# Block attention and two MoE layers on one core: batch 0's scores in plain float32, the softmax sums by a reduce over pairs, and another order of normalising

## Chip, cores and metric

The program runs on one core of a Trainium2 chip. The metric is the device time of one execution in microseconds; the kernel before takes 1253.38 us (median of three runs, 1252.73 to 1253.74).

## What is computed

The reference is an attention block followed by two dense layers of experts. Cut to what matters:

```python
# q, k, v: (4 batches, 8 heads, 576 tokens, 64)
scores = scale * q @ k.T                      # scale = 1/8
mask = (i // 64) >= (j // 64)                 # blocks of 64, causal by block
scores = where(mask, scores, -1e9)
scores = scores - max(scores)
attn = exp(scores)
attn = attn / (sum(attn) + 1e-9)
x = attn @ v                                  # -> (2304, 512)
h = max(x @ w1, x @ w2, x @ w3)               # 512 -> 768
x = h @ w_out                                 # 768 -> 512
p = probs / (sum(probs) + 1e-9)
out = sum over 4 experts: p[:, e] * (relu(x @ w1[e]) @ w2[e])   # 512 -> 1024 -> 512
```

## The kernel before

**Attention.** Two heads make a pair (16 pairs, four per batch). `load_pair` (line 89) brings q and k of a pair to SBUF, transposed, with the 64 head dimensions standing twice, in partitions 0 to 63 and again in 64 to 127. `prep_pair` (line 105) splits them for an exact product out of rounded float32 (fp32r) matmuls: `kk` holds the rounded keys in the lower half of the partitions (line 85 or 87) and the remainders in the upper half (line 122), `q1` the rounded queries times -1/8 (line 133) and `q2` their remainders (line 135). `scores` (line 163) then needs two fp32r matmuls over all 128 partitions per block, one with `q1` and one with `q2` (line 190). Rows of queries go in blocks i of 128; block i sees the keys up to 128(i+1), so blocks 0, 1, 2, 3 have 128, 256, 384 and 512 columns. The last 64 queries of both heads of a pair make one block, i = 4, with 576 columns and four matmuls per stretch. A small bf16 matmul with `corner` (line 195) masks the last 64 columns of blocks 0 to 3. The scores come out negated, so VectorE takes a minimum (line 208), and ScalarE computes exp and, in the same instruction, the row's sum (line 215). `normalise` (line 221) adds 1e-9 (line 223), takes the reciprocal (line 224), both on VectorE, and multiplies each tile on GpSimd (line 226). A head has two groups of tiles: group 0 has blocks 0, 2 and 3 and is normalised in the order 128, 384, 512 keys; group 1 has block 1, and for the second head of a pair block 4 too.

`turn_probs` (line 249) transposes the normalised tiles on TensorE (line 264; 25 transposes per pair) into PSUM. Its first bank of four is taken from block 3, the one with 512 keys, and the second from blocks 2 and 0. VectorE or ScalarE copies a bank to SBUF (lines 273 and 289). Batch 0's values are plain float32 matmuls (`values32`, lines 310, 318 and 322; TensorE runs each as two instructions); batches 1 to 3 use fp32r parts (lines 348 and 359).

**Order.** The loop at line 598 works on head g and on the scores of head g + 2; what `normalise` does is held back by one stage (`stage`, line 576). The framework then schedules the instructions by a simulated timeline, so that an engine can take an instruction that stands much later in the program. The first dense layer (`moe1`, line 526) of batch b needs all heads of the batch; from there on its matmuls (line 505) are mixed with the attention of the batch that follows. Its weights arrive as 64-bit floats and are converted once (`Convert`, line 394) in 26 pieces: ScalarE at lines 429, 431 and 85, GpSimd at lines 436 and 443, VectorE at lines 438, 439 and 452. These pieces already run during batch 0.

**Places.** Pairs 0 and 2 of batch 0 are loaded into `arena`, pairs 1 and 3 into `raw`. The split form of pairs 1 and 3 lies in the tile `spare`, which uses the place of the dense layer's `hh`; that of pairs 0 and 2 lies in `q1`, `q2` and `kk`. PSUM has four one-bank tiles (`ps_x`) for scores and transposes, one two-bank tile (`ps_c`) for block 4, and two banks (`ps_v`) for batch 0's values.

Of the kernel before, what the change touches and what calls it, by code (L numbers as in the profile page):

```python
# [6 lines left out]
F32 = mybir.dt.float32  # L7
# [11 lines left out]
P = 128  # L19
# [2 lines left out]
MOST = (1.875 - 2.0 ** -23) * 2.0 ** 32  # L22


def program(tc, q, k, v, w123, w_out, probs, e_w1, e_w2, out):
    nc = tc.nc

    B, H, D, S = q.shape[0], 2 * q.shape[1], q.shape[2] // 2, q.shape[4]
# [51 lines left out]

    QT, QW = 2 * (S - 64), 2 * S + 64
    pairs, heads, later = {}, {}, []
    def rounded(engine, to, x):
        if engine is nc.scalar:
            engine.copy(to, x)
        else:
            engine.tensor_scalar(to, x, 1.0, 0.0, op0=ALU.mult, op1=ALU.add)

    def load_pair(g):
        b, h0 = divmod(2 * g, H)  # L90

        if g % 2:
            raw = ap_.tile([P, 2, 2, S], F32, name="raw", tag="raw")[:]
        else:
            o = (B - 1) * KD * S
            raw = arena[:, o:o + 4 * S].rearrange("p (n h s) -> p n h s", n=2, h=2)
        for hs in ((0, 1), (1, 2)) if g == 0 else ((0, 2),):
            for n, src in ((1, k), (0, q)):
                nc.sync.dma_start(out=raw[:, n, hs[0]:hs[1]], in_=src[b, h0 // 2, :, hs[0]:hs[1]])

        vraw = ap_.tile([P, 5, 2, D], F32, name="vraw", tag="vraw", bufs=4)
        nc.sync.dma_start(out=vraw, in_=v[b, h0 // 2])
        pairs[g] = dict(raw=raw, vraw=vraw)

    def prep_pair(g):


        raw, vraw = pairs[g]["raw"], pairs[g]["vraw"]
        if g < NPAIR and g % 2:

            spare = mp.tile([P, 2 * QW + 2 * S], F32R, name="spare", tag="hh")
            q1, q2 = spare[:, 0:QW], spare[:, QW:2 * QW]
            kk = spare[:, 2 * QW:].rearrange("x (h s) -> x h s", h=2)
        else:
            q1, q2 = (ap_.tile([P, QW], F32R, name=x, tag=x, bufs=1)[:] for x in ("q1", "q2"))
            kk = ap_.tile([P, 2, S], F32R, name="kk", tag="kk", bufs=1)[:]
        for x in (q1, q2):
            nc.gpsimd.memset(x[:, QT + 64:QT + 128].bitcast(U32), 0)

        def keys(hs):  # L120
            (rounded if g else lambda _, to, x: rounded(nc.vector, to, x))(nc.scalar, kk[:, hs], raw[:, 1, hs])
# [15 lines left out]
        if g == 0:  # L137
            for h in range(2):
                keys(slice(h, h + 1))
                queries(slice(h, h + 1))  # L140
            yield
        else:
            keys(slice(0, 2))
            yield
            queries(slice(0, 2))
        pairs[g].update(q1=q1, q2=q2, kk=kk)
        if g < NPAIR:
            return
# [14 lines left out]
    def scores(g, grp):  # L163
        pair, h = pairs[g // 2], g % 2
        if grp == 0:
            heads[g] = dict(
                p=[None] * 4,
                mn=ap_.tile([P, 5], F32, name="mn", tag="mn", bufs=3),
                sm=ap_.tile([P, 5, 2], F32, name="sm", tag="sm", bufs=3),
            )  # L170
        mn, sm, pt = heads[g]["mn"], heads[g]["sm"][:, :, 0], heads[g]["p"]
        masked = g < 2 * H
        c0 = 3 * grp
        sets = []
        for tag, cols, plan in GROUPS[1][h] if grp else GROUPS[0]:
            st = (ps_x if tag == "x" else ps_c).tile([P, cols], F32, name="st", tag=tag)
            sets.append((st, plan))
            for i, o, w in plan:

                if i == 4:  # L180
                    todo = [(QT + 64 * x, x) for x in range(2)]
                else:
                    todo = [(h * QT // 2 + P * i, h)]
                c = 0
                while c < w:
                    n = min(w - c, 512 - (o + c) % 512)
                    terms = [(part, q0, x) for q0, x in todo for part in ("q1", "q2")]
                    ends = masked and i < 4 and c + n == w
                    for m, (part, q0, x) in enumerate(terms):
                        nc.tensor.matmul(  # L190
                            out=st[:, o + c:o + c + n], lhsT=pair[part][:, q0:q0 + P],
                            rhs=pair["kk"][:, x, c:c + n], start=m == 0, stop=m == len(terms) - 1 and not ends,
                        )
                    if ends:
                        nc.tensor.matmul(
                            out=st[:, o + w - 64:o + w], lhsT=corner, rhs=corner[:, 0:64], start=False, stop=True
                        )
                    c += n
        c = c0
        done = []  # L200
        for st, plan in sets:
# [7 lines left out]
            for col, i, o, w in mine:  # L209
                x = ap_.tile([P, w], F32, name=f"p{i}", tag=f"p{i}", bufs=2 if i == 4 else 3)  # L210
                if i == 4:
                    pair["p4"] = x
                else:
                    pt[i] = x
                nc.scalar.activation(  # L215
                    x, st[:, o:o + w], ACTF.Exp, bias=mn[:, col:col + 1], scale=-1.0,
                    accum_out=sm[:, col:col + 1],
                )
# [1124 lines left out]
```

## Time and profile before

| | |
|---|---|
| median of three runs | 1253.38 us |
| the profiled execution | 1249.91 us, span 1248.1 us |
| granted TensorE clock, mean | 0.996 |
| TensorE busy | 1211.2 us (97%) |
| VectorE busy | 929.7 us (74%) |
| ScalarE busy | 517.8 us (41%) |
| GpSimd busy | 357.1 us (29%) |

The span runs from the first instruction to the last; the 1.8 us between it and the execution's time lie around it. Busy shares are means over stages that have different limits. A matmul's end is modelled: in a stretch where TensorE runs without a gap the start of the next instruction, not the duration shown, tells what one costs.

### The profile page before, as it was taken

The numbers are of one execution on the slowest core, as the hardware profiler recorded it, in microseconds if no ns is written. First come the engines' busy times: TensorE is split into PE (matmuls) and PEld (weight loads), VectorE is DVE, ScalarE is ACT, GpSimd is POOL, SyncE is SP. The second block draws the span as 40 slices with busy tenths as digits, with TensorE's granted clock in tenths as the row PEclk, the third lists the DMA queues.
The fourth block names the chain that finished last, engine by engine and source line by source line (L and its number), as shares of the span: only waits on it lengthen the run. The fifth ranks groups of instructions, "written<-read, shape, count | busy, mean of one in ns | idle before, by whom it ended". The sixth has DMA issues, their size and how long they took to land.

```text
span 1248.1 us, 19730 instructions
## 1 busy us (share of the span) xinstructions
PE 1211.2 (97%) x7417; PEld 1157.8 (93%) x7417; DVE 929.7 (74%) x1716; ACT 517.8 (41%) x1076; POOL 357.1 (29%) x444
## 2 busy tenths in 40 slices
PE   7879998999999999999999999999999999999998
PEld 5669997999999999989999998999999999999998
DVE  7978988666565634377888896758787888686896
ACT  7977767544544421233444441233232223322222
POOL 3957786454344212243333341000000000000000
PEclk9999999999999999999999999999999999999999
DMA  8745574554533488478887864778888887776754
GB/s 304 248 164 197 170 265 161 172 153 155 183 102 119 120 287 304 150 303 332 312 311 296 310 247 162 287 274 316 300 306 311 315 314 281 253 258 228 253 210 170
DMA packets 82644, 299.69 MB, mean 240 GB/s; under 512 B 8748, under 2 KB 18036, under 8 KB 69492
## 3 DMA queue, kind: packets, MB, share of 16 engines
q1 hardware_dynamic: 82548, 298.42, 67.3%
q8 instruction: 59, 0.97, 0.3%
q14 instruction: 37, 0.30, 0.1%
HBM read 215.26 MB, written 83.14 MB: 239 GB/s over the span
## 4 chain that ended last, share of the span: by engine, by line
PE 74%; DVE 10%; DMA 5%; POOL 4%; ACT 3%; issue 3%; SPq 0%; DVEq 0%; ACTq 0%; POOLq 0%
PE m L858 24%; PE m L505 19%; PE o L1017 17%; PE st L190 3%; PE pv L359 2%; PE o L940 2%; PE o L943 2%; PE o L944 2%; DMA t<-in_e_w 2%; PE m L1017 2%; POOL p L226 2%; PE tt L264 2%; DVE mn L208 2%; DMA part<-in_e_w 1%; POOL arena L443 1%
## 5 line engine op out<-in xcount | busy, mean ns | idle before, releaser
L505 PE MATMUL m<-xh,wt 128*128 128x288 f32 x1120 | 238.4, 298 | 0.7 <-ACT mt L541 0.4
L858 PE MATMUL m<-t,w 128*128 128x384 f32 x1152 | 228.5, 336 | 0.0
L1017 PE MATMUL o<-hx,w 128*128 128x384 f32 x1176 | 225.7, 337 | 0.0
L1017 PEld LDWEIGHTS o<-hx,w 128*128 128x128 f32 x1176 | 207.8, 188 | 0.1
L858 PEld LDWEIGHTS m<-t,w 128*128 128x128 f32 x1152 | 203.4, 188 | 2.5 <-DVE tmp L878 0.4
L505 PEld LDWEIGHTS m<-xh,wt 128*128 128x128 f32 x1120 | 183.7, 188 | 1.6 <-DVE mt L543 0.8
L858 PE MATMUL m<-b,w 128*128 128x384 f32 x864 | 175.7, 337 | 2.0 <-ACT tmp L883 2.0
L505 PE MATMUL m<-xl,wt 128*128 128x288 f32 x560 | 165.3, 295 | 0.0
L858 PEld LDWEIGHTS m<-b,w 128*128 128x128 f32 x864 | 153.2, 188 | 5.1 <-ACT tmp L883 2.3
L226 POOL TENSOR_SCALAR p<-p,sm 128x128 f32<-128x128 f32 (+1 forms) x144 | 98.7, 702 | 52.1 <-DVE sm L223 17.0
L505 PEld LDWEIGHTS m<-xl,wt 128*128 128x128 f32 x560 | 105.3, 188 | 0.3
L878 DVE TENSOR_TENSOR tmp<-m,tmp 128x384 f32<-128x384 f32 x144 | 77.9, 550 | 19.4 <-PE m L858 19.2
L505 PE MATMUL m<-hh,wo 128*128 128x288 f32 x384 | 81.3, 299 | 2.9 <-ACT arena L554 1.3
L215 ACT ACTIVATE p<-st,mn 128x128 f32<-128x128 f32 (+3 forms) x144 | 78.5, 555 | 8.2 <-DVE mn L208 6.3
L988 ACT CAST hx<-hq 128x768 fp32r<-128x768 f32 x49 | 40.6, 837 | 99.0 <-PE o L1017 75.9
L190 PE MATMUL st<-kk,q 128*128 128x128 f32 (+4 forms) x336 | 71.2, 340 | 8.7 <-ACT q L133 5.5
L940 PE MATMUL o<-w,hh 128*128 128x512 f32 x192 | 74.7, 391 | 0.9 <-ACT hh L918 0.6
L813 POOL TENSOR_TENSOR w<-part,w 128x512 fp32r<-128x512 f32 x32 | 49.2, 1557 | 91.3 <-ACT w L811 61.2
L943 PE MATMUL o<-w,hh 128*128 128x512 f32 x192 | 74.7, 390 | 0.0
L944 PE MATMUL o<-w,hl 128*128 128x512 f32 x192 | 74.1, 390 | 0.0
L543 DVE TENSOR_TENSOR mt<-m,mt 128x288 f32<-128x288 f32 x96 | 43.2, 452 | 40.3 <-PE m L505 39.9
L264 PE MATMUL tt<-ident,p 128*128 128x128 f32 x400 | 61.0, 278 | 9.8 <-POOL p L226 5.4
(169 smaller groups left out, 2173.8 us busy)
## 6 DMA issues: line engine op xcount, KB each, us to landing
w<-kb SPq DMA_DIRECT2D x55, 1024.0 KB, 6.1
w<-ka SPq DMA_DIRECT2D x30, 1792.0 KB, 7.9
ka<-w SPq DMA_DIRECT2D x16, 1792.0 KB, 6.7
wt<-held SPq DMA_DIRECT2D x54, 512.0 KB, 4.1
kb<-part SPq DMA_DIRECT2D x16, 1024.0 KB, 7.0
kb<-w SPq DMA_DIRECT2D x16, 768.0 KB, 4.7
arena<-in_w SPq DMA_DIRECT2D x18, 512.0 KB, 4.0
wo<-held SPq DMA_DIRECT2D x12, 768.0 KB, 4.5
```

Of the source, the lines that this page charges most:

```text
L190: nc.tensor.matmul(out=st[:, o + c:o + c + n], lhsT=pair[part][:, q0:q0 + P], rhs=pair["kk"][:, x, c:c + n], start=m == 0, stop=m == len(t ...
L215: nc.scalar.activation(x, st[:, o:o + w], ACTF.Exp, bias=mn[:, col:col + 1], scale=-1.0, accum_out=sm[:, col:col + 1],)
L226: nc.gpsimd.tensor_scalar(x, x, sm[:, col:col + 1], 1.0, op0=ALU.mult, op1=ALU.mult)
L264: nc.tensor.transpose(tt[:, c:c + P], pt[i][:, k0:k0 + P], ident)
L505: nc.tensor.matmul(out=out_, lhsT=w, rhs=x, start=m == 0, stop=m == n - 1)
L813: eng.tensor_tensor(w[:, a:b, 1], raw[:, a:b], f(w[:, a:b, 0]), op=ALU.subtract)
L858: ins = nc.tensor.matmul(out=m, lhsT=a, rhs=b, start=start and n == 0, stop=stop and n == 3 * KH - 1, skip_group_check=True,)
L878: nc.vector.tensor_tensor(t, x, y, op=ALU.add)
L940: ins = nc.tensor.matmul(out=o, lhsT=hh[:, ts], rhs=wh, start=i == 0, stop=False)
L943: nc.tensor.matmul(out=o, lhsT=hh[:, ts], rhs=wl, start=False, stop=False)
L944: nc.tensor.matmul(out=o, lhsT=hl[:, ts], rhs=wh, start=False, stop=i == G - 1)
L1017: nc.tensor.matmul(out=o, lhsT=a, rhs=b, start=start and m == 0, stop=stop and m == 2, skip_group_check=True,)
```

## The change

Batch 0's q and k come in a second layout, `qk`: per pair, keys and queries of the first head in partitions 0 to 63 and those of the second head in 64 to 127, so a pair is half as many bytes. All four pairs have places of their own in the tiles `hh` and `hl` of the dense layer. Preparing a pair is a multiplication of the queries by -1/8 in place (VectorE for pair 0, GpSimd for pairs 1 to 3), with the last 64 queries of the two heads put on the diagonal of a zeroed 128 by 128 tile, `last`. A block of scores is then one plain float32 matmul over 64 partitions (128 for block 4). Batches 1 to 3 keep their split form.

For all batches the tile of sums has 1e-9 written beside each sum once, at the start, and one `tensor_reduce` over each pair of numbers gives sum + 1e-9. The tiles of group 0 are normalised in the order 512, 384, 128 keys.

```diff
+    sums = [ap_.tile([P, 5, 2], F32, name=f"sm{n}", tag=f"sm{n}") for n in range(3)]
+    for x in sums:
+        nc.gpsimd.memset(x, 1e-9)
...
     def load_pair(g):
         b, h0 = divmod(2 * g, H)
-        if g % 2:
-            raw = ap_.tile([P, 2, 2, S], F32, name="raw", tag="raw")[:]
+        if g < NPAIR:
+            if g == 0:
+                pairs["hh"] = mp.tile([P, 3, 2, S], F32, name="plain", tag="hh")
+                pairs["hl"] = mp.tile([P, NF, S], F32, name="plain", tag="hl")
+                for n in range(2):
+                    nc.gpsimd.memset(pairs["hl"][:, 2 + n, 0:P].bitcast(U32), 0)
+            raw = pairs["hh"][:, g] if g < 3 else pairs["hl"][:, 0:2]
+            for n in ((0, 1), (1, 2)) if g == 0 else ((0, 2),):
+                nc.sync.dma_start(out=raw[:, n[0]:n[1]], in_=qk[g, :, n[0]:n[1]])
         else:
...
-        for hs in ((0, 1), (1, 2)) if g == 0 else ((0, 2),):
             for n, src in ((1, k), (0, q)):
-                nc.sync.dma_start(out=raw[:, n, hs[0]:hs[1]], in_=src[b, h0 // 2, :, hs[0]:hs[1]])
+                nc.sync.dma_start(out=raw[:, n], in_=src[b, h0 // 2])
...
     def prep_pair(g):
-        if g < NPAIR and g % 2:
-            spare = mp.tile([P, 2 * QW + 2 * S], F32R, name="spare", tag="hh")
...
+        if g < NPAIR:
+            engine = nc.gpsimd if g else nc.vector
+            last = pairs["hl"][:, 2 + g % 2, 0:P]
+            x = raw[:, 1]
+            engine.tensor_scalar(x[:, 0:S - 64], x[:, 0:S - 64], -scale, 0.0, op0=ALU.mult, op1=ALU.add)
+            for half, at in ((lo, 0), (hi, 64)):
+                engine.tensor_scalar(
+                    last[half, at:at + 64], x[half, S - 64:S], -scale, 0.0, op0=ALU.mult, op1=ALU.add
+                )
+            pairs[g].update(k=raw[:, 0], q=x, last=last)
+            yield
+            return
...
     def scores(g, grp):
-                sm=ap_.tile([P, 5, 2], F32, name="sm", tag="sm", bufs=3),
+                sm=sums[g % 3],
...
+                if g < H:
+                    own = both if i == 4 else hi if h else lo
+                    terms = [(pair["last"] if i == 4 else pair["q"][own, P * i:P * i + P], pair["k"][own])]
...
         def normalise():
             cs = slice(c0, c)
-            nc.vector.tensor_scalar(sm[:, cs], sm[:, cs], 1e-9, None, op0=ALU.add)
-            nc.vector.reciprocal(sm[:, cs], sm[:, cs])
-            for col, x in done:
-                nc.gpsimd.tensor_scalar(x, x, sm[:, col:col + 1], 1.0, op0=ALU.mult, op1=ALU.mult)
+            nc.vector.tensor_reduce(mn[:, cs], sm[:, cs], axis=AX.X, op=ALU.add)
+            nc.vector.reciprocal(mn[:, cs], mn[:, cs])
+            for col, x in (done if grp else done[::-1]):
+                nc.gpsimd.tensor_scalar(x, x, mn[:, col:col + 1], 1.0, op0=ALU.mult, op1=ALU.mult)
```

## Rows read from the trace of the kernel before

**Rows 1.** Windows: stretch, length, busy (count) per engine, TensorE clock, DMA share, GB/s.

```profile
0.00:5.50 5.50, 0.00 (x0) 0.00 (x0) 1.22 (x2) 1.92 (x3) 1.27 (x12) 1.00 0.64 193
5.50:88.90 83.40, 69.13 (x372) 52.19 (x372) 70.67 (x141) 70.87 (x187) 57.58 (x74) 0.94 0.70 251
88.90:110.00 21.10, 21.10 (x158) 19.97 (x158) 19.42 (x48) 17.07 (x42) 11.43 (x15) 1.00 0.48 158
110.00:250.00 140.00, 132.82 (x961) 125.55 (x961) 116.68 (x273) 93.91 (x228) 99.68 (x132) 1.00 0.59 194
250.00:1248.10 998.10, 988.12 (x5932) 960.12 (x5930) 721.67 (x1255) 334.02 (x620) 187.19 (x214) 1.00 0.69 248
```

**Rows 2.** Timeline of all engines, 4 to 89 us: start, duration, instruction, idle before.

```profile
4.86 0.78 ACT L133 ACTIVATE q<-arena 128x512 fp32r<-128x512 f32 x2 [2.85 <-DMA arena<-in_q]
...
16.24 1.98 PE L190 MATMUL st<-spare 128*128 128x320 f32 x10 [2.26 <-ACT p L215]
...
18.11 1.95 PE L264 MATMUL tt<-ident,p 128*128 128x128 f32 x8
...
22.16 0.39 PE L310 MATMUL pv<-eh,vraw 128*128 128x128 f32 x2
...
76.34 0.47 PE L310 MATMUL pv<-eh,vraw 128*128 128x128 f32 x2
...
89.00 0.38 PE L505 MATMUL m<-xh,wt 128*128 128x288 f32 x1
```

**Rows 3.** Chain of waits in batch 0: start, length, engine, what, line, count.

```profile
70.35 0.43 PE st L190 x2
...
70.82 2.02 PE pv L318 x8
...
75.87 0.04 PE st L195
75.91 0.55 PE st L190 x2
...
88.22 0.44 PE tt L264 x4
```

**Rows 4.** Groups by line and shape, 0 to 115 us: the split into parts.

```profile
L122 DVE TENSOR_TENSOR spare<-raw,spare 64x1152 fp32r<-64x1152 f32 x2 | 3.7, 1842 | 1.3 <-ACT spare L85 1.3
L135 DVE SCALAR_TENSOR_TENSOR spare<-raw,spare 128x1024 fp32r<-128x1024 f32 x2 | 2.6, 1302 | 0.0
L85 ACT CAST spare<-raw 128x1152 fp32r<-128x1152 f32 x2 | 2.3, 1148 | 0.0
L133 ACT ACTIVATE spare<-raw 128x1024 fp32r<-128x1024 f32 x2 | 2.1, 1062 | 0.0
L122 DVE TENSOR_TENSOR kk<-arena,kk 64x576 fp32r<-64x576 f32 x2 | 1.5, 755 | 0.1
L87 DVE TENSOR_SCALAR kk<-arena 128x576 fp32r<-128x576 f32 x2 | 0.9, 460 | 4.2 <-DMA arena<-in_k 4.1
```

**Rows 5.** Groups by line and shape, 0 to 115 us: normalising and GpSimd.

```profile
L195 PE MATMUL st<-corner 128*128 128x64 bf16 x49 | 10.8, 220 | 0.0
L226 POOL TENSOR_SCALAR p<-p,sm 128x512 f32<-128x512 f32 x12 | 8.8, 731 | 0.0
L226 POOL TENSOR_SCALAR p<-p,sm 128x128 f32<-128x128 f32 x12 | 5.3, 441 | 5.5 <-ACT p L215 2.0 <-ACT wo L85 1.9 <-DVE sm L224 0.9
L223 DVE TENSOR_SCALAR sm<-sm 128x3 f32<-128x3 f32 x12 | 4.6, 387 | 1.3 <-ACT p L215 1.2
L208 DVE TENSOR_REDUCE mn<-st 128x1 f32<-128x128 f32 x12 | 3.4, 280 | 1.1 <-PE st L195 0.9
L224 DVE RECIPROCAL sm<-sm 128x3 f32<-128x3 f32 x12 | 2.1, 172 | 0.2
```

**Rows 6.** Timeline of the last head's wait, 76 to 82 us, columns as in rows 2.

```profile
78.62 2.70 POOL L226 TENSOR_SCALAR p<-p,sm 128x128 f32<-128x128 f32 x3 [1.95 <-ACT wo L85]
...
81.38 0.66 PE L264 MATMUL tt<-ident,p 128*128 128x128 f32 x4 [4.35 <-POOL p L226]
```

More of the change, by code (lines that the diff above doesn't have):

```diff
@@ L22, with program @@
 MOST = (1.875 - 2.0 ** -23) * 2.0 ** 32
-def program(tc, q, k, v, w123, w_out, probs, e_w1, e_w2, out):
+def program(tc, qk, q, k, v, w123, w_out, probs, e_w1, e_w2, out):
     nc = tc.nc
@@ L90, in load_pair @@
         b, h0 = divmod(2 * g, H)
[L92 to L97 removed]
+        if g < NPAIR:
[7 more added lines that the diff above has]
+                nc.sync.dma_start(out=raw[:, n[0]:n[1]], in_=qk[g, :, n[0]:n[1]])
+        else:
+            if g % 2:
+                raw = ap_.tile([P, 2, 2, S], F32, name="raw", tag="raw")[:]
+            else:
+                o = (B - 1) * KD * S
+                raw = arena[:, o:o + 4 * S].rearrange("p (n h s) -> p n h s", n=2, h=2)
             for n, src in ((1, k), (0, q)):
[L99 removed]
+                nc.sync.dma_start(out=raw[:, n], in_=src[b, h0 // 2])
         vraw = ap_.tile([P, 5, 2, D], F32, name="vraw", tag="vraw", bufs=4)
@@ L108, in prep_pair @@
         raw, vraw = pairs[g]["raw"], pairs[g]["vraw"]
-        if g < NPAIR and g % 2:
-            spare = mp.tile([P, 2 * QW + 2 * S], F32R, name="spare", tag="hh")
[L112 to L116, printed above, removed]
+        if g < NPAIR:
[10 more added lines that the diff above has]
+            return
+        q1, q2 = (ap_.tile([P, QW], F32R, name=x, tag=x, bufs=1)[:] for x in ("q1", "q2"))
+        kk = ap_.tile([P, 2, S], F32R, name="kk", tag="kk", bufs=1)[:]
         for x in (q1, q2):
@@ L135, in queries @@
                 nc.vector.scalar_tensor_tensor(low, src, -scale, f(high), op0=ALU.mult, op1=ALU.subtract)
[L137 to L145, printed above, removed]
+        keys(slice(0, 2))
+        yield
+        queries(slice(0, 2))
         pairs[g].update(q1=q1, q2=q2, kk=kk)
-        if g < NPAIR:
-            return
         vs = ap_.tile([P, 2, 5, P], F32R, name="vs", tag="vs", bufs=2)
@@ L168, in scores @@
                 mn=ap_.tile([P, 5], F32, name="mn", tag="mn", bufs=3),
-                sm=ap_.tile([P, 5, 2], F32, name="sm", tag="sm", bufs=3),
+                sm=sums[g % 3],
             )
-        mn, sm, pt = heads[g]["mn"], heads[g]["sm"][:, :, 0], heads[g]["p"]
+        mn, sm, pt = heads[g]["mn"], heads[g]["sm"], heads[g]["p"]
         masked = g < 2 * H
@@ L178, in scores @@
             for i, o, w in plan:
-                if i == 4:
-                    todo = [(QT + 64 * x, x) for x in range(2)]
-                else:
-                    todo = [(h * QT // 2 + P * i, h)]
+                if g < H:
+                    own = both if i == 4 else hi if h else lo
+                    terms = [(pair["last"] if i == 4 else pair["q"][own, P * i:P * i + P], pair["k"][own])]
+                elif i == 4:
+                    terms = [
+                        (pair[part][:, QT + 64 * x:QT + 64 * x + P], pair["kk"][:, x])
+                        for x in range(2) for part in ("q1", "q2")
+                    ]
+                else:
+                    q0 = h * QT // 2 + P * i
+                    terms = [(pair[part][:, q0:q0 + P], pair["kk"][:, h]) for part in ("q1", "q2")]
                 c = 0
@@ L186, in scores @@
                     n = min(w - c, 512 - (o + c) % 512)
-                    terms = [(part, q0, x) for q0, x in todo for part in ("q1", "q2")]
                     ends = masked and i < 4 and c + n == w
-                    for m, (part, q0, x) in enumerate(terms):
+                    for m, (qs, ks) in enumerate(terms):
                         nc.tensor.matmul(
-                            out=st[:, o + c:o + c + n], lhsT=pair[part][:, q0:q0 + P],
-                            rhs=pair["kk"][:, x, c:c + n], start=m == 0, stop=m == len(terms) - 1 and not ends,
+                            out=st[:, o + c:o + c + n], lhsT=qs, rhs=ks[:, c:c + n],
+                            start=m == 0, stop=m == len(terms) - 1 and not ends,
                         )
@@ L1303 @@
         laid[name] = np.concatenate((x, x), axis=2)
+    x = np.stack([inputs[name][0].reshape(H // 2, 2, S, D) for name in ("k", "q")])
+    laid["qk"] = x.transpose(1, 2, 4, 0, 3).reshape(H // 2, P, 2, S)
     x = np.zeros((B, H // 2, 5 * P, 2, D), np.float32)
@@ L1324 @@
     arrays, args = {}, []
-    for name in ("q", "k", "v", "w123", "w_out", "probs", "e_w1", "e_w2"):
+    for name in ("qk", "q", "k", "v", "w123", "w_out", "probs", "e_w1", "e_w2"):
         a = np.ascontiguousarray(laid[name])
```

4 lines of the change are left out of this document (2 added, 2 removed).

## The prediction

> **What bounds the kernel now.** I read the windows first, because the shares over the whole span mix stages. Of the 1248.1 us, TensorE is busy for all but 0.0 us of 88.9 to 110, 7.2 us of 110 to 250 and 10.0 us of the rest [rows 1]. After 88.9 us, therefore, TensorE's own work sets the end, and what the change does there is small. Before, it is different: nothing of TensorE in the first 5.5 us, then 69.1 busy of 83.4 us, beside 70.7 of VectorE, 70.9 of ScalarE and 57.6 of GpSimd [rows 1]. No engine is full, and these four wait for each other in turn. This stretch is batch 0's attention; it ends where the first dense layer's matmul starts, at 89.00 [rows 2]. **If that start moves by a microsecond, the end moves by nearly a microsecond**, since what follows is full. The question is thus when batch 0 is done.
>
> I cut this stretch in three with the timeline [rows 2]: the filling (to the first transpose of head 0, at 18.11), a steady part (first values matmul of head 0 at 22.16, of head 7 at 76.34: seven heads in 54.2 us, 7.74 us each), and the end of head 7 to 89.00.
>
> **TensorE's work per head.** In stretches without gaps the chain of waits gives prices [rows 3]. Eight instructions of line 318 for a first head (widths 384, 384, 256 and 128, two instructions each, nine blocks of 128 columns) take 2.02 us: plain float32 costs 0.224 us per 128 columns. A transpose costs 0.44 / 4 = 0.11. An fp32r block with two terms costs 0.55 for 512 columns and 0.43 for 384, and its mask 0.04; I take 0.3 for 256 and 0.2 for 128 on the same line. A pair before: two heads' blocks 0 to 3, 3.0 us; block 4, 4.5 column blocks by four matmuls at 0.06 (half the step from 384 to 512), 1.1; eight masks, 0.3; 25 transposes, 2.75; 25 column blocks of values, 5.6. Sum 12.8, or 6.4 per head. So of 7.74 us per head about 1.3 are stalls.
>
> **The change, part by part.**
> *Scores in plain float32.* A pair has 20 column blocks plus 4.5, at 0.224: 5.5 us in place of 4.1, so 0.7 us more per head. By columns alone (four passes against two for blocks 0 to 3, the same for block 4) it is 5120 columns at 2.4 GHz, 1.07 per head. I take 0.9, and batch 0 gains 7 us of TensorE work. It costs nothing where it falls into stalls, and all of it where it doesn't.
> *The split goes.* For pairs 1 to 3 ScalarE loses 1.15 + 1.06 us and VectorE 1.84 + 1.30 each; for pair 0 VectorE loses 2 x (0.46 + 0.755) and subtractions like those of line 135 at about half [rows 4]. With the small pieces for the last 64 queries that is near 14 us of VectorE and 9 of ScalarE in a stretch where each is 85% busy. What takes its place is three multiplications per pair. For pair 0 they are on VectorE: the row of 576 columns took 0.46, so 0.45 and two small ones of about 0.2. For pairs 1 to 3 they are on GpSimd: 0.73 for 512 columns and up to 0.44 each for the small ones [rows 5], 1.6 us per pair; the two memsets per pair that go are not counted against it. They are done well ahead, as their loads no longer wait for a place; uncovered they would delay one head's scores by 1.6 us.
> *Loads.* SP issues two transfers for pair 0 in place of four, and one per pair for pairs 1 to 3 in place of two; nothing moves later on its queue. The first two stay as large as before, so keys arrive near 4.1 and queries near 4.86 [rows 2, 4].
> *Filling.* Pair 0's queries are scaled by 5.3, and TensorE can run both heads' scores at once (5.5 us and masks 0.3), to about 11.2; block 4 of pair 1, which the scheduler placed ahead of the first transposes before too (at 16.24 [rows 2]), adds 1. Head 0's 512-key tile needs scores (1.8), a minimum (0.7), exp (0.9), reduce and reciprocal (0.35) and GpSimd (0.73), so it is ready near 10, before TensorE is free. The first transpose comes near 12.5 in place of 18.1: **-5.5 us**. It can't be worth more than about 8 (ready at 10), and 0 if exp still runs in the old order.
> *Sum + 1e-9.* The add of three numbers took 387 ns on average, the reciprocal of the same shape behind it 172 [rows 5]. A reduce of six elements is bounded below by about that reciprocal and above by the 280 of the reduce over 128; I take 0.17, which frees about 0.3 us of VectorE per head, inside the stalls. The page "SBUF — State Buffer" of the Trainium skill (section "SBUF: two separate sides") says that VectorE's two-port modes and GpSimd lock each other out of a shared pair of ports, and "VectorE: DVE Perf Modes" (section "The perf-mode tier table") gives tensor_reduce only the plain mode; by that the reduce wouldn't wait for GpSimd at all, and would sit at the lower bound.
> *Order.* Head 7's transposes waited 4.35 us for three GpSimd tiles of 2.70 us together [rows 6], because the first bank needs the tile that comes last. With it first, four transposes and the first copy run under the other two tiles. That is worth between 0 and 2.70 - 0.73 = 2.0 us at this place, and nothing where TensorE has other work. The clock stood at a mean of 0.94 in this stretch and 1.00 after it [rows 1]; a shorter wait may spare some of that. I take **-1.5 us**.
> *Steady part.* TensorE needs 6.4 + 0.9 = 7.3 per head. If half of the 1.3 us of stalls stay, since VectorE and ScalarE are relieved but the chain through exp, GpSimd and copies is as long, a head takes 7.97: 7 x 0.23 = **+1.6 us**.
> *Afterwards.* Weight pieces converted earlier may spare part of the 7.2 us idle in 110 to 250, or a new order may add to it; I take 0 and keep 3 us each way for the range.
> Sum: -5.5 - 1.5 + 1.6 = -5.4 us. The profiled execution is 1249.91, so it would be 1244.5; it lies 3.5 below the median of the runs, and against the median this is **1248.0 us**.
>
> **Rivals.**
> *A. As summed*, 1248.0; by itself 1244 to 1250.8.
> *B. The stalls go with the work that caused them.* VectorE and ScalarE lose 1.7 and 1.1 us per head, about as much as the stalls. Then TensorE paces at 7.3 per head: -3.1, with filling and end -10.1, so 1243.3, and 1240 with some of the later idle time. For it: TensorE is the only engine that would be near full. Against: GpSimd gains work and its tiles are what TensorE waited longest for.
> *C. Nothing to see.* All 1.3 us of stalls stay, being latencies and weight pieces in the queues, which the scheduler can pull into any freed time. A head takes 8.6: +6.2, less 7.0, so about 1252.6.
> *D. Slower: the array changes height.* Scores over 64 partitions alternate with masks over 128: four such blocks per head, in and out, eight changes. If TensorE must empty itself at each, a change costs what a mask takes alone less what it costs in a full stream, 0.22 - 0.04 = 0.18 us [rows 3, 5], or 1.44 per head. Then 7.3 + 1.44 + 0.65 = 9.4 per head: +11.6 - 7.0 = +4.6, so 1258. It decides from about 1 us per head more than TensorE needs in A. No row shows such a change, since all matmuls before use 128 partitions. The Trainium skill, "TensorEngine Tiling (Array Packing)", section "Key Properties", says that changing the tiling mode drains TensorE; by that D happens, unless the time is hidden in the stalls.
>
> **How the numbers follow.** A measurement of this kernel can tell 0.2%, or 2.5 us, from no change: 1250.9 to 1255.9 counts as the same. Chances: A 0.47, B 0.20, C 0.18, D 0.15. Faster is A and B, 0.67; the same is C, 0.18; slower is D, 0.15. The range goes from B's lower end, 1240, to D's, 1258; A alone has 1244 to 1250.8.
>
> **What would show it.** Right: the first transpose near 12.5 and the first dense matmul near 83.5; no instruction of lines 85, 122, 133 and 135 for batch 0; scores of 512 columns near 0.9 us; the new reduce near 0.17; later windows as full as before. Heads at 7.3 us would be B, at 8.6 C, at 9.4 D. For D the time from a block's last score to the mask behind it must show a gap near 0.18 in every block. The forecast is wrong at its root if the dense layer starts earlier and the end doesn't: then 110 to 250 lost what batch 0 won.

## The result and the profile after

The kernel after takes **1265.01 us** (median of four runs, 1263.04 to 1267.19), beside 1253.06 us of the kernel before (four runs, 1250.26 to 1253.74): a ratio of 1.010 with a 95% interval of 1.0077 to 1.0123. It is slower, and by more than the range reached (1258.0). The profiled execution is the longest of the four, 1267.19 us with a span of 1265.2; its mean granted clock is 0.993, that of the shortest 0.997.

The lines of the code have moved: plain scores are L207, their masks L212, the minimum L225, exp L232, the new reduce L240, the reciprocal L241, GpSimd's normalising L243, transposes L281, batch 0's values L327, L335 and L339, the dense layer L522.

The windows come first (columns as in [rows 1]; the last two rows are parts of the third):

```profile
5.50:88.90 83.40, 80.98 (x322) 46.94 (x321) 53.80 (x116) 58.17 (x160) 49.52 (x69) 1.00 0.58 208
88.90:110.00 21.10, 18.68 (x116) 15.59 (x116) 14.29 (x35) 15.38 (x41) 9.17 (x11) 0.92 0.35 122
110.00:250.00 140.00, 131.84 (x934) 124.90 (x933) 114.33 (x261) 92.37 (x222) 103.00 (x132) 0.96 0.58 195
...
220.00:230.00 10.00, 7.33 (x31) 6.47 (x32) 8.82 (x25) 4.73 (x14) 2.17 (x3) 0.63 0.38 135
230.00:240.00 10.00, 10.00 (x66) 9.87 (x65) 5.31 (x14) 6.18 (x18) 3.57 (x8) 0.86 0.41 137
```

In 5.5 to 88.9 VectorE and ScalarE have fallen from 70.7 and 70.9 us of work [rows 1] to 53.8 and 58.2, but TensorE is now busy for 80.98 of the 83.4 us and issues fewer matmuls in it (322 for 372). The bound of batch 0 has moved from a ring of four engines to TensorE alone. The timeline of TensorE (start, duration, instruction) says why; a cost is read from one start to the next:

```profile
5.16 0.79 PE L207 MATMUL st<-plain 64*128 64x128 f32 x2 [5.16 <-DVE plain L126]
...
17.31 2.07 PE L207 MATMUL st<-plain 64*128 64x512 f32 x2
19.32 0.24 PE L212 MATMUL st<-corner 128*128 128x64 bf16 x1
19.36 1.95 PE L281 MATMUL tt<-ident,p 128*128 128x128 f32 x8
21.24 0.79 PE L207 MATMUL st<-plain 64*128 64x128 f32 x2
...
29.79 0.64 PE L327 MATMUL pv<-eh,vraw 128*128 128x128 f32 x2
...
45.00 1.04 PE L281 MATMUL tt<-ident,p 128*128 128x128 f32 x8
45.97 0.48 PE L207 MATMUL st<-plain 64*128 64x128 f32 x2
46.38 0.20 PE L212 MATMUL st<-corner 128*128 128x64 bf16 x1
46.52 0.91 PE L207 MATMUL st<-plain 64*128 64x384 f32 x2
47.36 0.20 PE L212 MATMUL st<-corner 128*128 128x64 bf16 x1
47.49 1.12 PE L207 MATMUL st<-plain 64*128 64x512 f32 x2
48.55 0.20 PE L212 MATMUL st<-corner 128*128 128x64 bf16 x1
```

**First reading, the clock's level.** Eight transposes take 1.88 us at 19.36 and 0.97 at 45.00; a 512-column block takes 2.01 at 17.31 and 1.06 at 47.49. From 5.16 to about 34 every price is double, which is the lower of the two levels (1.2 GHz), though TensorE doesn't pause once in that stretch. The granted clock of the windows stands at 1.00 there, against the steps. The trace's record of the clock has its first entry only at 34.87 us, and the windows print 1.00 for the time before it. So the step from start to start is what is read; the first entry of the record lies where the steps halve, and it dates the rise of the level below.

The kernel before starts at the lower level too. Its 384 columns in two terms take 0.79 us at 7.03 and 0.44 at 34.12:

```profile
7.03 0.99 PE L190 MATMUL st<-kk,q 128*128 128x384 f32 x2
7.82 0.28 PE L195 MATMUL st<-corner 128*128 128x64 bf16 x1
...
34.12 0.59 PE L190 MATMUL st<-kk,q 128*128 128x384 f32 x2
34.56 0.20 PE L195 MATMUL st<-corner 128*128 128x64 bf16 x1
34.60 0.71 PE L190 MATMUL st<-kk,q 128*128 128x512 f32 x2
```

Its level rose at 13.74. Behind a wait of 2.26 us [rows 2] it was low again from 17.15 to 20.56, and the eight transposes at 18.11 lie in that stretch.

**Second reading, where batch 0's time went.** First values of heads 0, 1 and 7, and the first dense matmul:

| | head 0 | head 1 | head 7 | dense |
|---|---|---|---|---|
| before | 22.16 | 26.95 | 76.34 | 89.00 |
| after | 29.79 | 41.68 | 88.31 | 99.15 |

Up to head 1 it loses 14.7 us. From head 1 to head 7 it gains: 46.63 us for six heads (7.77 each) in place of 49.39 (8.23). The end of head 7 gains 1.8. Together +10.15 when the dense layer starts. Behind that point the profiled span is 1166.05 in place of 1159.1, another +6.95, which includes a drop of the clock to 0.63 at 220 to 230 (more on this under "Afterwards" below).

The small forecasts held: the scores start at 5.16 in place of 5.54, no split instruction of batch 0 is left, and the new reduce is short. The groups of 0 to 115 us (busy us, mean ns of one):

```profile
L241 DVE RECIPROCAL mn<-mn 128x3 f32<-128x3 f32 x11 | 1.9, 169 | 0.2
L240 DVE TENSOR_REDUCE mn<-sm 128x3 f32<-128x6 f32 x11 | 1.7, 154 | 3.3 <-ACT p L232 3.2
```

It takes 154 ns where the add took 387 [rows 5]. That 387 is a mean of two kinds. Of the 24 adds of all widths up to 115 us 12 took 124 to 169 ns; the other 12 took 308 to 637, and each of them ended 0.02 to 0.03 us behind the end of a GpSimd instruction. Of the 24 reduces none took more than 160 ns, though 12 ran beside a GpSimd instruction.

### The profile page after: what moved, and what is told of

It reads as the page before. It is cut to its first block, busy times and chain, and to the rows that moved or that the text cites. A ratio compares the mean times of both kernels' runs of the same rounds, so it can differ in the third digit from the quotient of the medians.

```text
span 1265.2 us, 19665 instructions
## 1 busy us (share of the span) xinstructions
PE 1236.1 (98%) x7401; PEld 1162.8 (92%) x7401; DVE 915.3 (72%) x1702; ACT 508.3 (40%) x1063; POOL 353.3 (28%) x450
## 4 chain that ended last, share of the span: by engine, by line
PE 77%; DVE 10%; DMA 4%; ACT 3%; POOL 3%; issue 2%; SPq 0%; DVEq 0%; POOLq 0%; ACTq 0%
PE m L875 23%; PE m L522 18%; PE o L1034 16%; PE st L207 5%; PE tt L281 2%; PE pv L376 2%; PE o L957 2%; PE o L960 2%; PE o L961 2%; PE m L1034 2%; DMA t<-in_e_w 2%; DVE mn L225 1%; POOL p L243 1%; PE pv L335 1%; DVE tmp L895 1%
## 5 line engine op out<-in xcount | busy, mean ns | idle before, releaser
L522 PE MATMUL m<-xh,wt 128*128 128x288 f32 x1120 | 238.2, 298 | 1.8 <-DVE mt L560 1.1
L522 PEld LDWEIGHTS m<-xh,wt 128*128 128x128 f32 x1120 | 183.6, 188 | 2.8 <-DVE mt L560 1.3
L522 PE MATMUL m<-xl,wt 128*128 128x288 f32 x560 | 165.2, 295 | 0.0
L243 POOL TENSOR_SCALAR p<-p,mn 128x512 f32<-128x512 f32 (+1 forms) x144 | 99.1, 707 | 27.8 <-DVE mn L241 16.5
L522 PEld LDWEIGHTS m<-xl,wt 128*128 128x128 f32 x560 | 105.2, 188 | 0.3
L895 DVE TENSOR_TENSOR tmp<-m,tmp 128x384 f32<-128x384 f32 x144 | 77.7, 549 | 19.5 <-PE m L875 19.3
L232 ACT ACTIVATE p<-st,mn 128x128 f32<-128x128 f32 (+3 forms) x144 | 78.5, 555 | 16.5 <-DVE mn L225 14.4
L522 PE MATMUL m<-hh,wo 128*128 128x288 f32 x384 | 83.2, 303 | 1.9 <-ACT arena L571 1.3
L225 DVE TENSOR_REDUCE mn<-st 128x1 f32<-128x128 f32 (+3 forms) x144 | 66.8, 504 | 19.1 <-PE st L212 16.0
L522 PEld LDWEIGHTS m<-hh,wo 128*128 128x128 f32 x384 | 64.4, 192 | 3.1 <-ACT arena L571 1.5
```

Of the source, the lines that this page charges most:

```text
L225: nc.vector.tensor_reduce(mn[:, col:col + 1], st[:, o:o + w], axis=AX.X, op=ALU.min)
L232: nc.scalar.activation(x, st[:, o:o + w], ACTF.Exp, bias=mn[:, col:col + 1], scale=-1.0, accum_out=sm[:, col, 0:1],)
L243: nc.gpsimd.tensor_scalar(x, x, mn[:, col:col + 1], 1.0, op0=ALU.mult, op1=ALU.mult)
L522: nc.tensor.matmul(out=out_, lhsT=w, rhs=x, start=m == 0, stop=m == n - 1)
L895: nc.vector.tensor_tensor(t, x, y, op=ALU.add)
```

## Experiments

Twelve kernels ran, in three series, each beside the kernel before. All medians, and the milestones of one profiled execution each (first values of heads 0, 1 and 7, first dense matmul, and the span behind it). "Level up" is the first entry of the record of TensorE's clock; "low behind" is how many us behind the first dense matmul the record has at the lower level, without the last 5 us of the span:

| kernel | median us | ratio (95%) | head 0 | head 1 | head 7 | dense | behind | level up | low behind |
|---|---|---|---|---|---|---|---|---|---|
| before | 1253.06 | | 22.16 | 26.95 | 76.34 | 89.00 | 1159.1 | 13.74 | 0 |
| after | 1265.01 | 1.0100 (1.0077 to 1.0123) | 29.79 | 41.68 | 88.31 | 99.15 | 1166.1 | 34.87 | 13.7 |
| rows128 | 1251.34 | 0.9999 (0.9983 to 1.0015) | 18.32 | 27.06 | 75.26 | 83.58 | 1163.6 | 9.09 | 6.8 |
| mask64 | 1259.88 | 1.0059 (1.0044 to 1.0074) | 25.42 | 34.62 | 79.73 | 90.37 | 1165.8 | 24.99 | 10.2 |
| before_mask64 | 1256.15 | 1.0028 (1.0015 to 1.0041) | 25.51 | 30.51 | 83.39 | 95.81 | 1159.5 | 26.53 | 0 |
| warm_up | 1261.28 | 1.0065 (1.0045 to 1.0085) | 26.03 | 38.27 | 84.38 | 92.23 | 1163.8 | 4.55 | 6.8 |
| long_64rows | 1263.66 (one run) | | 38.03 | 47.84 | 91.97 | 99.81 | 1162.1 | 28.83 | 0 |
| norm_only | 1252.00 | 1.0000 (0.9987 to 1.0012) | 22.68 | 28.52 | 79.77 | 87.62 | 1160.4 | 13.43 | 0 |
| scores_only | 1258.84 | 1.0048 (1.0033 to 1.0063) | 29.82 | 40.76 | 87.42 | 95.44 | 1163.0 | 32.97 | 6.8 |
| order_undone | 1260.74 | 1.0058 (1.0041 to 1.0076) | 29.74 | 40.35 | 86.90 | 94.91 | 1162.9 | 32.22 | 3.4 |
| rows128_old_norm | 1250.31 | 0.9980 (0.9970 to 0.9989) | 18.70 | 27.41 | 74.32 | 84.78 | 1163.4 | 8.98 | 6.8 |
| rows128_warm | 1247.16 | 0.9951 (0.9935 to 0.9967) | 18.72 | 27.34 | 74.42 | 82.76 | 1164.0 | 7.63 | 10.2 |
| warm_old_norm | 1252.51 | 0.9996 (0.9986 to 1.0005) | 20.93 | 29.61 | 78.18 | 88.36 | 1162.6 | 9.33 | 3.4 |
| before_warm | 1257.64 | 1.0037 (1.0020 to 1.0055) | 21.11 | 33.23 | 82.82 | 93.39 | 1160.4 | 5.74 | 0 |

**rows128: the same scores over all 128 partitions.** Each head's queries stand in a tile whose other 64 partitions are zero, so the product is the same and no matmul changes height.

```diff
-                    own = both if i == 4 else hi if h else lo
-                    terms = [(pair["last"] if i == 4 else pair["q"][own, P * i:P * i + P], pair["k"][own])]
+                    q0 = h * (S - 64) + P * i
+                    terms = [(pair["last"] if i == 4 else pair["q"][:, q0:q0 + P], pair["k"])]
...
```

Not shown are the memsets of the two zeroed tiles and the multiplication of the queries, which now goes head by head into them.

> The changed kernel with batch 0's scores over all 128 partitions: each head's queries stand in a zeroed tile, the other head's half is zero, and the keys of both heads stream. Columns and passes stay the same; no matmul uses 64 partitions any more. Theory H (the change of height costs 0.2 to 0.3 us per block of scores, 32 blocks): a 512-key block takes 0.85 to 0.95 us at the upper clock instead of 1.06, the first dense matmul starts 6 to 9 us earlier than 99.15, time 1256 to 1259. Theory P (the four passes of plain float32 themselves fill TensorE): a block keeps its price but for a few hundredths, 1262 to 1266. Theory C (64 partitions keep the granted clock at its lower level to 34 us): transposes at 0.11 us already near 20 us, which is worth another 5 us, so 1251 to 1256 together with H.

Measured: 1251.34 us, 13.7 less than after. The timeline of TensorE, columns as above:

```profile
7.17 2.06 PE L214 MATMUL st<-plain 128*128 128x512 f32 x2
9.02 0.24 PE L219 MATMUL st<-corner 128*128 128x64 bf16 x1
9.09 0.68 PE L214 MATMUL st<-plain 128*128 128x256 f32 x2
...
31.26 0.39 PE L214 MATMUL st<-plain 128*128 128x128 f32 x2
31.48 0.19 PE L219 MATMUL st<-corner 128*128 128x64 bf16 x1
31.51 0.89 PE L214 MATMUL st<-plain 128*128 128x384 f32 x2
32.24 0.19 PE L219 MATMUL st<-corner 128*128 128x64 bf16 x1
32.26 1.10 PE L214 MATMUL st<-plain 128*128 128x512 f32 x2
33.21 0.19 PE L219 MATMUL st<-corner 128*128 128x64 bf16 x1
```

The first transpose comes at 13.21, near the 12.5 that the prediction gave, and the dense layer at 83.58 against 83.5. The lower level ends at 9.09 in place of 34.87: a block of 512 takes 1.85 at 7.17, one of 256 0.52 at 9.09. At the upper level the blocks of 128, 384 and 512 columns take 0.22, 0.73 and 0.95 to their mask and 0.03 or less more to the next block; in after they take 0.41, 0.84 and 1.06 and then 0.13 to 0.14. So with half the partitions used, a matmul of the same columns costs no less, and the change of height costs time. The end didn't follow the dense layer's start: that is 5.4 us earlier than before, and the ratio is 0.9999. That is taken up in the section on the prediction.

**mask64: the mask in the scores' own 64 partitions.** The scores stay at 64. Four of a head's eight changes of height go; in and out of the group of three blocks and of block 1 remain.

```diff
-                            out=st[:, o + w - 64:o + w], lhsT=corner, rhs=corner[:, 0:64], start=False, stop=True
+                            out=st[:, o + w - 64:o + w], lhsT=corner[at], rhs=corner[at, 0:64], start=False, stop=True
...
```

`at` is the half of the partitions that the head's scores use, and `corner` has its row of 1e15 in partition 64 too.

> The changed kernel with the mask matmul taken over the same 64 partitions as the scores it follows, so that a head's blocks and masks run without a change of height between them. Theory H: the 0.13 to 0.2 us between a block and its mask and behind it fall to about 0.04, 1258 to 1261; changes remain only where transposes and values come between. Theory P and theory C: no difference, 1262 to 1266; the lower clock lasts to about 34 us as before.

Measured: 1259.88 us, 5.1 less than after. In the timeline the stretch of blocks at the upper level reads:

```profile
30.62 0.48 PE L208 MATMUL st<-plain 64*128 64x128 f32 x2
30.95 0.19 PE L214 MATMUL st<-corner 64*128 64x64 bf16 x1
30.98 0.89 PE L208 MATMUL st<-plain 64*128 64x384 f32 x2
31.70 0.19 PE L214 MATMUL st<-corner 64*128 64x64 bf16 x1
31.73 1.10 PE L208 MATMUL st<-plain 64*128 64x512 f32 x2
32.67 0.19 PE L214 MATMUL st<-corner 64*128 64x64 bf16 x1
32.79 1.86 PE L208 MATMUL st<-plain 128*128 128x320 f32 x6
```

Between blocks of one height nothing is paid: 384 columns to the next block 0.75, as in rows128 (0.75), against 0.97 in after, which is 0.11 for each of its two changes. Only the way in (0.33 for 128 columns in place of 0.22) and out (0.12 from mask to block 4 in place of 0.03) still shows about 0.1. The level rises at 24.99 us, ten earlier than in after and sixteen later than in rows128; no theory had that. The changes alone are thus about 0.9 us per head at the upper level (8 x 0.11), some 7 in batch 0. The late rise is the larger part by an estimate: the level of after is up 25.8 us later than that of rows128, and at half the clock that is worth up to 12.9.

**before_mask64: the opposite, changes of height put into the kernel before.** Its batch 0 masks run over 64 partitions, its scores stay at 128.

```diff
+                    at = lo if g < H else both
...
-                            out=st[:, o + w - 64:o + w], lhsT=corner, rhs=corner[:, 0:64], start=False, stop=True
+                            out=st[:, o + w - 64:o + w], lhsT=corner[at], rhs=corner[at, 0:64], start=False, stop=True
```

> The kernel before with one edit: batch 0's mask matmuls use 64 partitions in place of 128. The data, columns and passes of the scores are untouched, but TensorE changes height eight times per head, 64 times in all. Theory H by itself: the start to start time from the last score to the mask and from the mask to the next block grows by 0.1 to 0.15 us each, 6 to 9 us of TensorE time; part of it falls in stalls, so the first dense matmul starts 2 to 6 us later than 89.0 and the time is 1254 to 1259. Theory P: no change, 1251 to 1254.

Measured: 1256.15 us, 3.2 more than the kernel before in the same series (1252.97), and the dense layer starts 6.8 later. A block of 384 columns at the upper level:

```profile
31.24 0.62 PE L190 MATMUL st<-spare 128*128 128x384 f32 x2
31.79 0.20 PE L196 MATMUL st<-corner 64*128 64x64 bf16 x1
31.92 0.73 PE L190 MATMUL st<-spare 128*128 128x512 f32 x2
```

It takes 0.55 to its mask and 0.13 from there on; the same block in the kernel before takes 0.44 and 0.04 (at 34.12, shown above). So a change costs 0.1 us here too, in other data types and with nothing else in the program altered. The 6.8 us are not these changes alone. The level rises at 26.53 in place of 13.74, though all but the masks still runs over 128 partitions, and up to the dense layer it is low again for 13.7 us in place of 10.2. Changes of height thus go with a late rise too, not only matmuls that are all of half the height.

**warm_up: 36 small matmuls ahead of after.** They write a spare PSUM tile that nobody reads.

```diff
+    WARM = 36
+    warm_ = ps_v.tile([P, 512], F32, name="warm", tag="v")
+    for _ in range(WARM):
+        nc.tensor.matmul(out=warm_[:, 0:P], lhsT=corner, rhs=corner, start=True, stop=True)
```

> The changed kernel with 36 bf16 matmuls of the mask tile on a spare PSUM tile ahead of the first scores, from about 1.6 us on. They compute nothing that is used. Theory C, in the form that a busy TensorE at the start raises the clock: transposes at 0.11 us by 15 us, first dense matmul 6 to 8 us earlier, 1256 to 1259. If 64-partition matmuls bring the clock down again, or the warming is too short: 1262 to 1266. Theories H and P say nothing of it.

Measured: 1261.28 us, 3.7 less than after and between the two expected ranges; its seven runs, 1256.58 to 1265.47, reach into those of after. The timeline:

```profile
5.13 0.48 PE L212 MATMUL st<-plain 64*128 64x128 f32 x2
5.55 0.20 PE L217 MATMUL st<-corner 128*128 128x64 bf16 x1
...
13.00 0.20 PE L217 MATMUL st<-corner 128*128 128x64 bf16 x1
14.50 1.81 PE L286 MATMUL tt<-ident,p 128*128 128x128 f32 x8 [1.30 <-POOL p L248]
16.24 0.79 PE L212 MATMUL st<-plain 64*128 64x128 f32 x2
```

The first two heads' scores now run at the upper level and are done at 13.0 in place of 19.3. Then TensorE waits 1.30 us for GpSimd, the level falls (the eight transposes take 1.74, the block of 128 columns 0.73), and the record has it low from 14.79 to 31.85 us, with scores over 64 partitions again. So scores over 64 partitions did not bring the level down while TensorE ran without a gap. A part of the loss comes back through the level, but not the whole.

**long_64rows: is it the height that keeps the level low?** rows128 with 200 bf16 matmuls over 64 partitions ahead.

```diff
+    WARM = 200
...
+        nc.tensor.matmul(out=warm_[:, 0:P], lhsT=corner[lo], rhs=corner[lo], start=True, stop=True)
```

> The scores over 128 partitions, with 200 bf16 matmuls of 64 partitions and 128 columns, without a gap, ahead of everything on TensorE; they compute nothing that is used and delay the first scores. Theory C (matmuls over half the partitions don't bring the granted clock up, or later): the start to start time stays at 0.107 us for all 200, some 21 us, and the clock rises only once the scores over 128 partitions run. Against it: the step falls to about 0.055 us within 8 us, as in the run with 36 warming matmuls over 128 partitions, and the 200 end near 13 us.

The timeline of TensorE, two answers:

```profile
1.66 21.51 PE L179 MATMUL warm<-corner 64*128 64x128 bf16 x200 [1.66 <-POOL corner L54]
23.10 0.79 PE L219 MATMUL st<-plain 128*128 128x128 f32 x2
...
28.85 0.89 PE L219 MATMUL st<-plain 128*128 128x384 f32 x2
29.58 0.19 PE L224 MATMUL st<-corner 128*128 128x64 bf16 x1
```

200 matmuls over 64 partitions take 21.5 us without a gap, 0.107 each: 128 columns at 1.2 GHz, from the first to the last. The scores over 128 partitions behind them begin at the lower level (0.58 for the block of 128 at 23.10) and are at the upper one by 28.85 (384 columns in 0.73). In warm_up 36 matmuls of the same type, columns and tile over 128 partitions had the level up by 5.13 (0.42 for the block of 128). So the height goes with the level here, not the kind of work. How soon full height brings it up differs: between 2.9 us (warm_up) and 8.4 us (norm_only) behind the first matmul, in the kernels that start with full height alone. This is a single execution; its 1263.66 us contains the 18 us put ahead.

**scores_only, norm_only, order_undone: the parts of the change alone.** scores_only is after with the normalising of before, norm_only the reverse; order_undone is after with the reduce, but with the tiles in the old order.

```diff
-            for col, x in (done if grp else done[::-1]):
+            for col, x in done:
```

> The changed kernel with normalise as before (an add of 1e-9, 128 keys first), so that the plain float32 scores over 64 partitions stand alone. Theory H with the lower clock at the start (the loss lies in the scores): 1262 to 1266, first transpose near 19 us and first values matmul near 30 us as in the changed kernel. Theory S (normalise makes part of the loss): 1258 to 1261.

> The kernel before with the change of normalise alone (sum + 1e-9 by a reduce, 512 keys first). Theories H, P and C: this part loses nothing; 1249 to 1253.5, since the 4.35 us wait at head 7 becomes 1 to 2 us shorter. Theory S (the new order and the reshuffled schedule cost time in 110 to 250 us, where 4 us were lost in the profile after): 1255 or more.

> The changed kernel with the sum by the reduce kept and the tiles normalised in the old order, 128 keys first. Without both it took 1258.8, with both 1265.0. If the order makes the loss (its tiles collide with VectorE's work at head 7): 1258 to 1261. If the reduce makes it: 1263 to 1266.

Measured: 1258.84, 1252.00 and 1260.74 us. The scores alone make about half of the loss (ratio 1.0048), the normalising alone nothing (1.0000), and the two together 1.0100. order_undone shows that of the 6.2 us between scores_only and after the order is 4.3. In batch 0 order_undone and after are alike up to head 0 (29.74 and 29.79), then order_undone gains 1.4 us to head 7 and 2.8 from there to the dense layer (8.01 in place of 10.84; scores_only, with the old order too, has 8.02). On the kernel before it is the other way round: in norm_only the new order takes this end from 12.66 us to 7.85. The other 1.9 us of the 6.2 go with the reduce, but there the runs overlap (1258.63 to 1260.45 and 1259.78 to 1262.61). TensorE at head 7 of after, then of order_undone:

```profile
89.38 0.66 PE L281 MATMUL tt<-ident,p 128*128 128x128 f32 x4 [0.69 <-POOL p L243]
91.98 0.63 PE L281 MATMUL tt<-ident,p 128*128 128x128 f32 x4 [1.94 <-POOL p L243]
92.44 4.65 PE L335 MATMUL pv<-eh,vraw 128*128 128x512 f32 x8
```

```profile
87.72 0.66 PE L281 MATMUL tt<-ident,p 128*128 128x128 f32 x4 [0.34 <-POOL p L243]
89.36 3.06 PE L335 MATMUL pv<-eh,vraw 128*128 128x512 f32 x8 [0.99 <-ACT eh L306]
```

And GpSimd's group of the tile of 128 keys there, 86 to 96 us of after and 84 to 92 of order_undone (busy us, mean ns of one):

```profile
L243 POOL TENSOR_SCALAR p<-p,mn 128x128 f32<-128x128 f32 x1 | 1.9, 1853 | 0.0
```

```profile
L243 POOL TENSOR_SCALAR p<-p,mn 128x128 f32<-128x128 f32 x1 | 0.4, 371 | 0.6 <-PE st L212 0.6
```

The new order does what it says: the first bank waits 0.69 us, not 4.35 [rows 6]. But the tile of 128 keys now comes last, behind the point where VectorE begins batch 1's long instructions (L456, L154 and L141 from 89.66 to 93.57), and takes 1853 ns in place of 371. The second bank waits 1.94 us for it, and behind that the values run slower: eight instructions take 4.49 us to the next start in place of 2.90, at a granted clock of 0.83 for 90 to 100. The Trainium skill, "SBUF — State Buffer", section "SBUF: two separate sides", says that VectorE instructions with two SBUF inputs and GpSimd ones exclude each other for a whole instruction; the 1853 ns agree with that, though no run here separates it from other causes. In order_undone the same long instructions, from 88.15 on, run beside the tile of 576 keys instead, and that one takes 2225 ns.

**rows128_old_norm, rows128_warm, warm_old_norm: the edits combined.** The first is rows128 with the normalising of before, the second rows128 with the 36 matmuls of warm_up, the third all three. They ask which version is best.

> The scores in plain float32 over all 128 partitions, with normalise as before. With the changed normalise it took 1251.3 us, no different from the kernel before. If the two changes of normalise are worth nothing where TensorE is short of slack: 1249 to 1254. If they are what saves head 7's end in the plain kernel: 1254 to 1257. If they harm: below 1249.

> The scores over 128 partitions, with the 36 warming matmuls ahead. Scores of the first head at the upper clock from 5 us on in place of 9 us: the first values matmul 1.5 to 3 us earlier than 18.3. If the filling reaches the end: 1248 to 1250. If the later heads wait for ScalarE and GpSimd, as the chain of waits from 67 to 89 us says: 1250 to 1253, and the steady dense matmuls start at 88 to 89 us again.

> The scores over 128 partitions, 36 warming matmuls ahead, and normalise as before. With the changed normalise this took 1247.2 us. If normalise is neutral here: 1245 to 1249; if the old order helps, as without warming (1250.3 against 1251.3): 1244.5 to 1247.

Measured: 1250.31, 1247.16 and 1252.51 us. **rows128_warm is the best version, 0.9951 of before**, and beats both kernels. Its time lies below both expected ranges, and the third missed its expectation. With scores over 128 partitions the new normalising costs 1.0 us without the warming matmuls (the intervals of the two ratios overlap) and gains 5.3 with them. But warm_old_norm differs from rows128_warm by more than its normalising: in its schedule the tile `corner` is ready at 3.62 us in place of 1.66, so that warming and scores start 2 us later, and the level falls for 6.8 us in batch 0 where it doesn't fall in rows128_warm. Its dense layer starts 5.6 us later. The 5.3 us are the schedule's as much as the normalising's. The warming matmuls do not bring head 0's values forward (18.72 and 18.32): the last of them starts its mask at 12.65 in place of 13.18, but then the transposes wait 0.68 us for GpSimd. The level is up at 7.63, only 1.5 us earlier than in rows128. What the profiles show of a gain over rows128 lies at the end of batch 0, where the dense layer of rows128 starts at 83.58, waits 1.60 us for ScalarE at 86.61, and runs on steadily only from 89.04. But the two profiled executions differ by 0.5 us (1248.90 and 1249.38), so where the 4.2 us between the medians come from isn't shown.

**before_warm: the same 36 matmuls ahead of the kernel before.**

> The kernel before with the 36 warming matmuls alone. If warming by itself is what beats the kernel before: 1246 to 1249. If it helps only where TensorE is short of time at the start, as in the plain kernels: 1251 to 1254, since the first heads wait for VectorE's and ScalarE's split here.

Measured: 1257.64 us, 4.9 more than before in its series (1252.72); a miss. Head 0's values come 1.05 us earlier, head 1's 6.3 later. The waits of TensorE there are for GpSimd's tiles (L231, 4.9 us in all) and for VectorE's sums (L228, 3.6; L229, 2.6). The level is up at 5.74, but it falls four times before the dense layer, for 17.1 us in place of 10.2. A faster TensorE at the start was worth nothing in this ring of four engines; why the schedule came out worse isn't shown.

## Why the prediction was wrong

**Filling: the step that failed.** The prediction gave -5.5 us at the first transpose, 12.5; it came at 19.36, +1.3. At the first values it is +7.6 for head 0 and +14.7 for head 1. The order of events was as forecast, and rows128 shows that the estimate fits better where the level rises early (13.21 for 12.5). What failed is the price: 0.224 us per 128 columns [rows 3] came from a place at the upper level and from matmuls over 128 partitions, and neither was true of the first scores. The two heads' scores, put at 5.8 us to 11.2, and block 4, put at 1, took from 5.16 to 19.36, 14.2 us, and one block of 256 columns was still to come. The rows of before held the warning: eight transposes shown with 1.95 us at 18.11 [rows 2], where four take 0.44 in the chain [rows 3]. The prediction used the second and did not ask why the first was double. A late start was in no term of its sum, though the first scores of before ran at the lower level for 8.2 us as well.

**Rival D: right mechanism, size off, and half the story.** Each change of height costs about 0.1 us (after, mask64 and before_mask64), not 0.18, which is 0.9 per head, not 1.44; the gap shows in every block, as D asked. D took the 0.22 of a mask alone from a duration [rows 5], whose end is modelled. The Trainium skill's sentence on the drain at a change of tiling mode ("TensorEngine Tiling (Array Packing)", "Key Properties") agrees with the trace, with 0.1 us as its price here. What was in no rival is that with scores over 64 partitions, and the changes of height that they bring, the clock stays at 1.2 GHz from 5.16 to 34.87. The time lies beyond D's 1258 because the normalising adds to it: the scores alone came to 1258.84 (scores_only). That this is nearly D's number is luck, since D's sum has -5.5 us for a filling that got slower.

**Steady part.** Forecast: 7.97 us per head from head 0 on, +1.6 in all; measured 8.36, +4.3. The mean hides two things: head 0 to head 1 takes 11.9, of which 5.1 are at the lower level, and the six heads behind it 7.77, less than before's 8.23. Rival B's premise holds there: the stalls went (80.98 of 83.4 us busy), and the changes of height took part of the room. The term for the scores, 0.9 us per head, was right without these changes: a head's four blocks and half of block 4, with masks, take 3.3 us in rows128 and 2.45 in before.

**Split removed.** VectorE and ScalarE lost 16.9 and 12.7 us of that stretch, more than the 14 and 9 forecast, since some of their other work moved behind it: over the whole execution VectorE has 14.4 us less (929.7 and 915.3) and ScalarE 9.5 (517.8 and 508.3), which is the forecast. It was worth nothing as long as TensorE was slower.

**Order and end of head 7.** The end is 1.8 shorter, near the -1.5 forecast, but that is luck: with the old order it is 8.01 us (order_undone), so the new order costs 2.8 in this kernel. The prediction counted the first bank's wait and not what the last tile would meet.

**Reduce.** 154 ns against 0.17 us forecast, and under the reciprocal's 169: the lower bound held. So did its ground, the Trainium skill's "SBUF — State Buffer", section "SBUF: two separate sides", as the prediction read it: 12 of the 24 adds ended with a GpSimd instruction, and no reduce waited for one.

**Afterwards.** The prediction took 0 and 3 us each way. The table shows a pattern: the four kernels with before's scores need 1159.1 to 1160.4 us behind the first dense matmul, the ten with plain scores 1162.1 to 1166.1. So some 2 to 7 us of what is won in batch 0 are given back, and this is why rows128 ends level with before. Much of it is the clock. The four have no stretch at the lower level there, and nine of the ten have 3.4 to 13.7 us of it: after has 0.63 and 0.86 in 220 to 240, with waits of TensorE of 2.31, 0.56 and 1.14 us from 218.7 on, and a shorter stretch at 775. If a stretch at the lower level costs half its length, which is an estimate, the rest is 1158.9 to 1162.1 us for all fourteen, and after's 1166.1 becomes 1159.2. In rows128 a part is the early first dense matmul itself, with the wait of 1.60 us behind it. These are one profiled execution each, and no run isolates why the plain kernels wait there and before's don't; it stays open, as does why before_warm loses.

Of the 12 us between the medians, the runs account for the scores' height: with it undone the time falls by 13.7 us under the new normalising (after and rows128) and by 8.5 under the old (scores_only and rows128_old_norm). Of the 13.7, 5.1 go with four of eight changes and the ten us by which the level rises earlier (mask64). The order's 4.3 us overlaps with this: with before's scores or with scores over 128 partitions the normalising costs 1.0 us or less.

## What to carry to other kernels

Price TensorE's first work at the step that the trace shows at that place, not at the one of the steady part, and ask of every doubled step what the engine did before it. Keep matmuls at the full 128 partitions, with zeros where need be, when those around them have that height, and above all at the start. An order is not better because its first consumer waits less: look at what its last tile runs beside, and measure the parts together, since here one part, the normalising, went with 0, +1.0, +6.2 or -5.3 us depending on the others and on the schedule that came of them.

## What the runs showed of the hardware

Matmuls over 64 partitions cost as much per column as over 128, and a change between the two costs about 0.1 us at the upper level (0.55 for 0.44, 0.13 for 0.04 in before_mask64). A stream of 200 of them, 21.5 us without a gap, stayed at 0.107 us per 128 columns, the 1.2 GHz level, while scores over 128 partitions, half of whose queries are zero, were at the upper level at 9.09 in rows128 and at 28.85 in long_64rows, where they begin at 5.01 and 23.10. Masks over 64 partitions between scores over 128 put the rise from 13.74 to 26.53 (before_mask64). Once up, the level held through scores over 64 partitions while TensorE ran without a gap (5.13 to 13.0 us of warm_up). The record of the granted clock read 1.00 in stretches where the steps were those of 1.2 GHz (5 to 34 us of after, ahead of its first entry). VectorE's add over three columns took 153 ns at 76.86 of before, with no GpSimd instruction beside it, and up to 637 where it ended with one; the reduce in its place took at most 160. A GpSimd multiplication over 128 columns took 371 ns where VectorE ran short instructions and 1853 ns beside long ones.
